# Attention and a feed-forward layer on one core: the second stage by 1024 tokens, with seven block products in place of eight and weights read from DRAM

## The chip, the cores and the metric

The kernel runs on one core of a Trainium2 chip. The metric is the device time of one execution in microseconds; three runs of the kernel before stand here, and their median is the time before. Engines are named as in the profile: PE (TensorE, matmuls), PEld (its weight loads), DVE (VectorE), ACT (ScalarE), POOL (GpSimd), SP (SyncE, which here only issues DMAs). ACT and POOL can issue DMAs too; those instructions stand in the engine's own queue, behind and ahead of its other work.

## What is computed

```python
# attention: batch 8, heads 8, 576 positions, head size 64, band of 64
scores = scale * q @ k.T                       # scale = 1/8
scores = where(0 <= pos_i - pos_j < 64, scores, -1e9)
attn = exp(scores - max(scores)); attn = attn / (sum(attn) + 1e-9)
x = (attn @ v) as (8 * 576 tokens, 512)
# feed-forward
h = x @ w_in                                   # 512 -> 2048
out = maximum(0.01 * h, h) @ w_out             # 2048 -> 512
```

All in fp32; w_in and w_out come as 64-bit floats, handed over as integers. There are 4608 tokens.

## The kernel before

**Feed-forward.** The tokens are nine chunks of 512 (`CH`), and d_ff is 16 blocks of 128 (`FT`, index f). Every fp32 operand of these two products is split in a high and a low part of the type f32r, and one product is three matmuls: high by high, high by low, low by high. A step (c, f) is `mm1` (L529: 4 × 3 = 12 matmuls 128x512 at L539 into one PSUM bank h) and `mm2` (L574: 12 matmuls at L586, three for each of the four accumulators, 128 tokens each, that stay in PSUM for all 16 f). Between the two stand `leak` (ACT, L544, the leaky ReLU out of PSUM), `high` (ACT, L550, the cast to f32r) and `low` (DVE, L554, the rest). `mm2` of a step is issued behind `mm1` of the next. `evict` (L597) moves the four sums out; SP writes them.

**Weights.** Each of the 32 blocks comes as 512 KB of 64-bit words (tile `raw`, the issue at L175 on ACT's queue, the first three on SP's) and is turned into singles by DVE and ACT, step by step: `bits`, `sign`, `abs`, `clamp`, `join`, then `split` (L210, high part, ACT) and `rest` (L214, low part, DVE). High and low parts of all 32 stay in SBUF to the end, 4 × 512 singles per partition and f.

**Attention.** A unit m is two blocks of 64 queries with all heads. Scores are computed transposed, keys on partitions, so that the maximum and the sum over the keys go across partitions. In the late loop, for the pair m, m + 1:

- `scores_3` (L467): the scores of a unit on PE, 32 matmuls (L239)
- `shield_3` (L472): scale and mask, DVE, L477, two per unit, out of PSUM
- `most_3` (L481): the maximum by `partition_all_reduce` on POOL, L486, two per unit
- `exps_3` (L489): minus the maximum (DVE, L492), exponential (ACT, L493), two each
- `sums_3` (L495): the sum by the same instruction on POOL, L497, two per unit
- `fold_3` (L499): 1e-9 added and the reciprocal of 128x512 (DVE, L501 to L503)
- `values_3` (L505): attn @ v on PE, 16 matmuls (L512)
- `product_3` (L518), `low_3` (L523): the product with the reciprocals (DVE, L520), cast (ACT, L521) and low part (DVE, L526), straight into x of the chunk in SBUF

**Order.** The opening is a list of names written out by hand (`ORDER`): weight conversion, the first attention units and 19 first steps. Then come 16 jobs, chunks 0 and 1 with f from 8 to 15, with the rest of the conversion woven in. Then the late loop over `steps`, chunks 2 to 8 by 16 f: every eight steps one pair of units is computed, 24 units (12 to 35) in the first 96 steps; the scores of both units stand behind the second of the eight steps, the values of both behind the sixth. Every engine issues in the order of this code.

Chunks 0 and 1, and the attention before unit 12, are the same before and after.

Of the kernel before, what the change touches and what calls it, by code (L numbers as in the profile page):

```python
# [13 lines left out]
F32 = mybir.dt.float32  # L14
# [17 lines left out]
UPC = CH // QB  # L32
UNITS = 2
TURNED = 2 * UPC
PAIRED = 12
PACE = 5
ROOMS = 3
# [35 lines left out]
"""  # L73
KT = DM // P
# [14 lines left out]
def band_attention_ffn(ctx: ExitStack, tc: tile.TileContext, qT, kB, vW, vL, w_in, w_out, eye_mask, out):  # L89
# [3 lines left out]
    xp = ctx.enter_context(tc.tile_pool(name="xp", bufs=2))  # L93
# [7 lines left out]


# [12 lines left out]
    room = [wk.tile([P, 4 * 512], F32, tag=f"late{FT - 1 - i}", bufs=1, name=f"room{i}") for i in range(ROOMS)]  # L115
# [24 lines left out]
    def load_q(m):  # L140
        if m < NU // 2:
            nc.sync.dma_start(q_of(m), qT[m])

    def load_k(m):
        if m < NU // 2:
            nc.sync.dma_start(k_of(m), kB[m])

    def load_v(m):
        if m < NU // 2:
            nc.sync.dma_start(v_of(m), vL[m - PAIRED] if m >= PAIRED else vW[m])  # L150
# [8 lines left out]

    wi = [[const.tile([P, KT, P], F32R, name=f"wi{f}_{i}") for i in range(2)] for f in range(FT - ROOMS)]  # L160
    wo = [[const.tile([P, DM], F32R, name=f"wo{f}_{i}") for i in range(2)] for f in range(FT - ROOMS)]

    def late_weights(f):
        t = wk.tile([P, 4, 512], F32R, tag=f"late{f}", bufs=1, name=f"w{f}")
        wi.append([t[:, i].rearrange("p (a b) -> p a b", a=KT) for i in range(2)])
        wo.append([t[:, 2 + i] for i in range(2)])

# [41 lines left out]
    def split(n):  # L209
        nc.scalar.copy(flat(parts(n)[0]), singles[n])  # L210

# [7 lines left out]
    def x_of(u):  # L219
        c, w = divmod(u, UPC)  # L220
        if c not in xs:
            xs[c] = [xp.tile([P, KT, CH], F32R, tag=f"x{i}", name=f"x{i}_{c}") for i in range(2)]
        return [x[:, :, w * QB : (w + UNITS) * QB] for x in xs[c]]

# [63 lines left out]
    def top(b):  # L288
        if 0 < b < OWN:
            mx = more_mx[b - 1]  # L290
        else:
            mx = wk.tile([P, 512], F32, tag="pT", bufs=1, name=f"mx{b}")
# [98 lines left out]
    def most(u, j):  # L391
        mx = wk.tile([P, 512], F32, tag="pT", bufs=1, name=f"mx{u}_{j}")
# [62 lines left out]
    def open_room():  # L455
# [3 lines left out]
        k = flat(wk.tile([P, NP, 2, D], F32, tag="y", bufs=1, name="late_k").rearrange("p a b c -> p a (b c)"))  # L459
        later.update(e=e, n=n, v=v, k=k.rearrange("p (a b c) -> p a b c", a=UNITS, b=NP))  # L460

# [3 lines left out]
    def scores_3(m):  # L465
        ps = [bank(t, f"s{m}_{j}") for j, t in enumerate((next(of_h), next(of_h)) if m % 2 else "st")]
        quarter_scores(m, ps, False)  # L467
        probs[m] = ps

    def shield_3(m):  # L470
        ps = probs.pop(m)
        a = mask_of(UNITS * m).bitcast(F32)  # L472
        n = a.shape[1]
        a = flat(a)[:, None, :].broadcast_to([P, H // n, n * QB])
        for j in range(2):
            e, s = (x.rearrange("a (b c) -> a b c", c=n * QB) for x in (e_of(m)[:, j], ps[j]))
            nc.vector.scalar_tensor_tensor(e, s, SCALE, a, ALU.mult, ALU.add)  # L477

    def spare(name):
        return wk.tile([P, 512], F32, tag="pT", bufs=1, name=name)  # L480

    def most_3(m):
        for j in range(2):
            b = 2 * (m % 2) + j
            mx = later["n"][:, b - 1] if b in (1, 2) else spare(f"mx{m}_{j}")
            nc.gpsimd.partition_all_reduce(mx, e_of(m)[:, j], P, ReduceOp.max)  # L486
            probs[m, j] = mx

    def exps_3(m):  # L489
        for j in range(2):  # L490
            e = e_of(m)[:, j]
            nc.vector.tensor_tensor(e, e, probs.pop((m, j)), ALU.subtract)  # L492
            nc.scalar.activation(e, e, AF.Exp)  # L493

    def sums_3(m, j):  # L495
        t = probs[m, "sum"] = spare(f"n{m}") if j else later["n"][:, m % 2]
        nc.gpsimd.partition_all_reduce(t, e_of(m)[:, j], P, ReduceOp.add)  # L497

    def fold_3(m):  # L499
        r, t = later["n"][:, m % 2], probs.pop((m, "sum"))  # L500
        nc.vector.tensor_scalar_add(r[64:], t[64:], 1e-9)  # L501
        nc.vector.tensor_scalar_add(r[:64], r[:64], 1e-9)
        nc.vector.reciprocal(r, r)  # L503

    def values_3(m):  # L505
        ps = bank("st"[m % 2], f"o{m}")
        for w in range(UNITS):
            v = v_heads(m, w)
            for p in range(NP):
                for j in range(2):  # L510
                    c = (2 * p + w) * QB
                    nc.tensor.matmul(  # L512
                        ps[64 * j : 64 * j + 64, c : c + QB], v[:, 2 * p + j], e_of(m)[:, j, c : c + QB],
                        start=True, stop=True,
                    )
        probs[m] = ps

    def product_3(m):  # L518
        r = later["n"][:, m % 2]
        nc.vector.tensor_tensor(r, probs.pop(m), r, ALU.mult)  # L520
        nc.scalar.copy(x_of(UNITS * m)[0], r.rearrange("a (b c) -> a b c", b=NP))  # L521

# [4 lines left out]

    g = {}  # L530

    def mm1(c, f, part):

# [270 lines left out]
```

## Time and profile before

| | |
|---|---|
| runs | 897.09, 896.88, 896.97 us (median 896.97) |
| profiled execution, first to last instruction (span) | 895.8 us |
| busy: PE, PEld | 887.6, 730.1 us |
| busy: DVE, ACT, POOL | 498.1, 304.8, 315.0 us |
| granted PE clock | full in all slices |
| moved by DMA | 68.48 MB, 56.43 read from and 11.01 written to DRAM |
| chain that ended last: PE | 98% |

The time of a run is measured around the whole program; the span of the profiled execution is the time from its first to its last instruction, which is 1.2 us less than the median of the runs. Rows that group instructions read: line, engine, operation, output<-inputs, count | busy us, mean ns of one | idle time of that engine just before, and what ended most of it. The chain of waits is followed back from the last instruction; a row there is start, length, engine, tile, line and count. A row of the DMA view reads: issue line and queue, tile, count and nanoseconds of one issue.

### The profile page before, as it was taken

The page shows a single profiled execution, that of the slowest core. Times are in us where ns is not written, and L with a number is a line of the kernel's source. Part 1 is how long each engine was busy: PE and PEld are TensorE (multiplying, and loading weights), DVE is VectorE, ACT ScalarE, POOL GpSimd, SP SyncE. Part 2 cuts the span into 40 slices and gives each one's busy share as a digit, 9 for nine tenths or more (in the row PEclk, how much of TensorE's full clock was granted, in tenths as well). Part 3 has the DMA queues.
Part 4 walks back from the last instruction along what each step waited for, and adds up shares of the span by engine and source line. Part 5 has one row for each costly group of instructions (what it writes and reads, how often), then busy time and mean ns, then how long its engine had stood idle before and what let it go on. Part 6 is the DMA issues. An engine that isn't in the chain of part 4 may idle for free.

```text
span 895.8 us, 16193 instructions
## 1 busy us (share of the span) xinstructions
PE 887.6 (99%) x7018; PEld 730.1 (82%) x7018; DVE 498.1 (56%) x650; ACT 304.8 (34%) x517; POOL 315.0 (35%) x132
## 2 busy tenths in 40 slices
PE   8999999999999999999999999999999999999998
PEld 5887888888888888888888888888888888888886
DVE  7999774597473636465464737373636455461111
ACT  4666554232222333233322242223323322323222
POOL 5332000674351708080625335351708071620000
PEclk9999999999999999999999999999999999999999
DMA  8663623233311111011211121112101211001001
GB/s 326 207 212 121 221 93 120 72 109 129 106 48 45 50 56 62 26 48 71 72 48 48 48 95 48 48 49 87 55 5 64 75 48 48 2 1 48 0 1 48
DMA packets 30359, 68.48 MB, mean 76 GB/s; under 512 B 3024, under 2 KB 3152, under 8 KB 30288
## 3 DMA queue, kind: packets, MB, share of 16 engines
q1 hardware_dynamic: 25824, 51.75, 16.5%
q10 hardware_dynamic: 4464, 15.70, 5.3%
q8 instruction: 55, 0.90, 0.4%
q14 instruction: 16, 0.13, 0.0%
HBM read 56.43 MB, written 11.01 MB: 75 GB/s over the span
## 4 chain that ended last, share of the span: by engine, by line
PE 98%; POOL 0%; DMA 0%; ACT 0%; issue 0%; DVE 0%; ACTq 0%
PE acc L586 45%; PE h L539 44%; PE s L239 4%; PE o L512 3%; PE o L328 1%; PE o L424 0%; DMA k<-kB 0%; PE s L273 0%; PE t L354 0%; PE s L307 0%; POOL mx L293 0%; POOL room L293 0%; DVE e L283 0%; ACT e L314 0%; ACT e L312 0%
## 5 line engine op out<-in xcount | busy, mean ns | idle before, releaser
L539 PE MATMUL h<-x,wi 128*128 128x512 f32 (+1 forms) x1440 | 337.1, 384 | 0.5 <-ACT g L544 0.5
L539 PEld LDWEIGHTS h<-x,wi 128*128 128x128 f32 x1440 | 265.6, 188 | 54.4 <-ACT g L544 0.7
L586 PE MATMUL acc<-wo,gh 128*128 128x512 f32 x936 | 292.6, 394 | 0.0
L554 DVE TENSOR_TENSOR gl<-g,gh 128x512 fp32r<-128x512 f32 (+1 forms) x147 | 107.5, 732 | 332.7 <-ACT gh L550 332.3
L586 PEld LDWEIGHTS acc<-wo,gh 128*128 128x128 f32 x936 | 172.8, 188 | 36.4
L544 ACT ACTIVATE g<-h 128x512 f32<-128x512 f32 (+1 forms) x147 | 86.4, 588 | 330.8 <-PE h L539 324.1
L586 PE MATMUL acc<-wo,gl 128*128 128x512 f32 x468 | 182.4, 390 | 0.0
L486 POOL PARTITION_ALL_REDUCE mx<-e x12 | 21.4, 1782 | 307.6 <-DVE e L477 307.6
L586 PEld LDWEIGHTS acc<-wo,gl 128*128 128x128 f32 x468 | 87.9, 188 | 18.6
L550 ACT CAST gh<-g 128x512 fp32r<-128x512 f32 (+1 forms) x147 | 90.0, 612 | 10.6 <-PE acc L586 6.3
L503 DVE RECIPROCAL late_n<-late_n 128x512 f32<-128x512 f32 x24 | 80.5, 3353 | 0.8
L539 PE MATMUL h<-x,w 128*128 128x512 f32 x324 | 77.8, 389 | 0.0
L539 PEld LDWEIGHTS h<-x,w 128*128 128x128 f32 x324 | 60.8, 188 | 12.6
L586 PE MATMUL acc<-w,gh 128*128 128x512 f32 x216 | 66.7, 390 | 0.0
L497 POOL PARTITION_ALL_REDUCE late_n<-e x12 | 38.8, 3233 | 25.7 <-ACT late_e L493 25.7
L493 ACT ACTIVATE e<-e 128x512 f32<-128x512 f32 x24 | 15.2, 632 | 95.4 <-DVE e L492 95.4
L586 PEld LDWEIGHTS acc<-w,gh 128*128 128x128 f32 x216 | 40.5, 188 | 8.4
L393 POOL PARTITION_ALL_REDUCE mx<-e x8 | 15.2, 1898 | 90.3 <-DVE e L385 87.0
L586 PE MATMUL acc<-w,gl 128*128 128x512 f32 x108 | 42.0, 389 | 0.0
L293 POOL PARTITION_ALL_REDUCE mx<-e x13 | 25.7, 1977 | 45.1 <-ACT e L285 28.3
L497 POOL PARTITION_ALL_REDUCE n<-late_e x12 | 41.5, 3460 | 0.0
L497 POOL PARTITION_ALL_REDUCE late_n<-late_e x12 | 40.9, 3405 | 0.0
(99 smaller groups left out, 825.7 us busy)
## 6 DMA issues: line engine op xcount, KB each, us to landing
q<-qT SPq DMA_DIRECT2D x34, 256.0 KB, 3.4
raw<-w_out ACTq DMA_DIRECT2D x15, 512.0 KB, 3.3
out<-o SPq DMA_DIRECT2D x30, 256.0 KB, 2.1
raw<-w_in ACTq DMA_DIRECT2D x14, 512.0 KB, 3.3
k<-kB SPq DMA_DIRECT2D x25, 256.0 KB, 3.6
v<-vL SPq DMA_DIRECT2D x12, 512.0 KB, 3.8
late_v<-vL SPq DMA_DIRECT2D x12, 512.0 KB, 4.2
v<-vW SPq DMA_DIRECT2D x8, 520.0 KB, 5.6
```

The costliest lines, as they stand in the source:

```text
L239: nc.tensor.matmul(ps[j][t, c : c + QB], k[i][s, p], q[s, w, p], start=not begun and (not more or (w, p) == (0, 0)), stop=not begun and no ...
L293: nc.gpsimd.partition_all_reduce(mx, probs[b], P, ReduceOp.max)
L393: nc.gpsimd.partition_all_reduce(mx, probs_of[:, j], P, ReduceOp.max)
L486: nc.gpsimd.partition_all_reduce(mx, e_of(m)[:, j], P, ReduceOp.max)
L497: nc.gpsimd.partition_all_reduce(t, e_of(m)[:, j], P, ReduceOp.add)
L503: nc.vector.reciprocal(r, r)
L512: nc.tensor.matmul(ps[64 * j : 64 * j + 64, c : c + QB], v[:, 2 * p + j], e_of(m)[:, j, c : c + QB], start=True, stop=True,)
L539: nc.tensor.matmul(ps, a[:, k, :], b[:, k, part], start=n == 0, stop=n == len(terms) - 1)
L544: nc.scalar.activation(t[0], ps, AF.Prelu, alpha=0.01)
L550: nc.scalar.copy(g[c, f, part.start][0][:, part], t[0])
L554: nc.vector.tensor_tensor(lo, t[0], hi.bitcast(F32), ALU.subtract)
L586: nc.tensor.matmul(acc[c, i], a[:, ts], b, start=begin and n == 0, stop=end and n == 2)
```

## The change

Chunks 0, 1 and 2 (`LEAD = 3`) are computed as before, chunk 2 under new lines (`early_first`, `early_second`) and with the order of f turned so that 15, 14, 13 and 12 come first. The other 3072 tokens go in three turns (`NS`) of 1024.

**Seven products.** x of a turn is cut in 2 × 2 blocks (512 tokens by 256 of d_model), w_in for a pair f, f + 8 in 2 × 2 (256 of d_model by 128). The four blocks of h are put together from seven products (Winograd's form of Strassen's scheme), each of 6 matmuls: `product`, L1103. The combinations of x (`x_build`, L936, DVE) and of w_in (`prep`, L1045) are made ahead; those of the products are made by `put` (ACT, L1109) and five additions per f on DVE (`add`, L1112: one operand from PSUM, one from SBUF); then four leaky ReLUs per f on ACT (L1115, `leaky`). An accumulator bank is used again two or three products later, and waits until the addition from it is done. After the eight f come the casts (`high`, L1118), low parts (`low`, L1121, 32 per turn, DVE) and `second`: 2 halves × 16 f × 12 matmuls, as many as before, whose output is transposed (`outT`, put right on the host by a transposition).

**Weights from DRAM.** `split` also stores the single-precision w_in (16 stores of 256 KB, ACT's queue). During the jobs n = 7 to 15, SP stores the parts of the weights that the turns use unchanged (24 × 256 KB and 16 × 512 KB). In chunk 2 and turn 0, ACT's queue reads singles back, DVE and ACT make the combined blocks, and ACT's queue stores them (eight times, L1042 to L1055). The slots in SBUF that had held weights then serve for other things; a ring of four slots of 1 MB is filled by DMAs that POOL issues (`fill`, L1090: 30 per turn, each read by 24 matmuls). Each fill waits until PE is done with the slot.

**Attention through DRAM.** Scores (L268) and values (L849) of units 12 to 35 go one unit at a time. Of the sums over the keys only one row is kept, as 128x8; DVE takes the reciprocals of that (L826, L827), and SP's DMAs write them to DRAM and spread them over the partitions. The products (L860) are stored to DRAM by unit, and x of a turn is read from there. For units 12 to 19 the sum is not on POOL but on PE: four matmuls with ones (`add_of`, L808), copied out by ACT. The loads of q, k and v move from SP's to ACT's queue. All attention ends within turn 0.

**Order.** From chunk 2 on, the order on each engine is set by a planner (`arrange`) that gets each operation with an engine, a cost, what it waits for and a rank, and always issues what is ready first, by rank.

POOL, in the late loop before; L486 is the maximum, L497 the sum of a pair of units:

```order
L497 ISA late_n<-e 128x512 [waits DVE_49,Activation_49,Pool_49]
L497 ISA n_5544<-e 128x512 [waits Activation_49,Pool_49]
L497 ISA late_n<-late_e 128x512 [waits Activation_49]
L497 ISA n_5600<-late_e 128x512 [waits DVE_49,Activation_49]
L486 ISA mx_0_5906<-e 128x512 [waits DVE_49,Pool_49]
```

POOL, in the change, around the end of chunk 2 and the start of turn 0; L787 is a maximum or a sum, L1090 a fill of the ring:

```order
L1090 DMA p_27_3509<-w_first 128x2048 [waits DMAHW0_49,DMAHW1_49,DMASW1_49,PE_49]
L787 ISA g<-late_e 128x512 [waits Activation_49]
L787 ISA late_o_2495<-e 128x512 [waits DMAHW3_49]
L1090 DMA p_28_3600<-w_first 128x2048 [waits DMAHW2_49,DMAHW7_49,DMASW2_49,PE_49]
L787 ISA late_o_2496<-e 128x512 [waits DMAHW7_49]
L787 ISA late_o_2495<-e 128x512 [waits Activation_49]
L1090 DMA p_29_3724<-w_first 128x2048 [waits DMAHW0_49,DMAHW2_49,DMASW3_49,PE_49]
```

Fills now stand between the reduces, about two reduces to a fill, and each waits for PE and for DMAs; a reduce behind it in the queue waits with it.

DVE, in the late loop before: low parts of steps (L554), the reciprocals of a unit (L501 to L503) and its product (L520):

```order
L554 TENSOR_TENSOR gl_12_0_6398<-g_12_0_6395,gh_12_0_6397 128x512
L501 TENSOR_SCALAR late_n<-n_6348 64x512
L502 TENSOR_SCALAR late_n<-late_n 64x512
L503 RECIPROCAL late_n<-late_n 128x512
L554 TENSOR_TENSOR gl_13_0_6434<-g_13_0_6431,gh_13_0_6433 128x512
L520 TENSOR_TENSOR late_n<-o_6437,late_n 128x512
```

DVE, in the change, from the end of chunk 2 into turn 0: the last low parts of x (L955), then additions of the first seven products (L1112) among the steps of attention units (L781 mask, L791 minus the maximum, L860 product, L826 and L827 reciprocals):

```order
L955 TENSOR_TENSOR pfew_3354<-p_23_2886,pfew_3354 128x4x2x128
L791 TENSOR_TENSOR e<-e,late_o_2496 128x512
L1112 TENSOR_TENSOR pxa_30_3976<-m_0_1_3969,pxa_30_3976 128x512
L781 SCALAR_TENSOR_TENSOR e<-s_0_3912,away 128x512
L860 TENSOR_TENSOR late_n<-o_3829,late_n 128x512
L1112 TENSOR_TENSOR pxa_30_3976<-m_0_2_3998,pxa_30_3976 128x512
L781 SCALAR_TENSOR_TENSOR e<-s_1_3913,away 128x512
L1112 TENSOR_TENSOR p_31_4027<-m_0_3_4007,pxa_30_3976 128x512
L791 TENSOR_TENSOR late_e<-late_e,g 128x512
L826 TENSOR_SCALAR c_2423<-c_2423 128x8
L827 RECIPROCAL c_2423<-c_2423 128x8
```

The additions from PSUM stand behind a mask, a subtraction or a product of attention, and x's last low parts directly ahead of the first of them; a reciprocal is one of 128x8 in place of 128x512.

The core of the diff, cut:

```python
+LEAD = 3
+NS = (NCHUNK - LEAD) // 2
+KEPT = 7
...
     def split(n):
         nc.scalar.copy(flat(parts(n)[0]), singles[n])
+        if n % 2 == 0:
+            nc.scalar.dma_start(w_single[n // 2], singles[n])
...
+        if n >= KEPT:
+            for f in kept[(n - KEPT) * len(kept) // (len(jobs) - KEPT) : (n - KEPT + 1) * len(kept) // (len(jobs) - KEPT)]:
+                f()
...
-    steps = [(c, f) for c in range(2, NCHUNK) for f in range(FT)]
-    for n, (c, f) in enumerate(steps):
...
+    def add_of(m):
+        ps = bank("s", f"sum{m}")
+        for c in range(2):
+            for j in range(2):
+                q = 32 * (2 * j + c)
+                nc.tensor.matmul(
+                    ps[q : q + 32, :256], ones(), e_of(m)[:, j, 256 * c : 256 * c + 256], start=True, stop=True,
+                    tile_position=(0, q),
+                )
...
+    def fill(n, of):
+        ring[n] = hold(RING_AT[n % RING], F32R)
+        nc.gpsimd.dma_start(ring[n], of.rearrange("p a b -> p (a b)"))
...
+    def product(n, part, k, name):
+        b, begin = BANK[k], k < 4
+        if begin:
+            tiles[b] = ps_o.tile([P, 512], F32, tag=f"o{b}", name=name)
+        w, x = ring[n][:, 512 * part : 512 * (part + 1)], [x_part(OF_X[k], j) for j in range(2)]
+        terms = [(kt, i, j) for kt in range(2) for i, j in ((0, 0), (0, 1), (1, 0))]
+        for c, (kt, i, j) in enumerate(terms):
+            nc.tensor.matmul(
+                tiles[b], w[:, 256 * i + 128 * kt : 256 * i + 128 * kt + 128], x[j][:, 512 * kt : 512 * kt + 512],
+                start=begin and c == 0, stop=c == len(terms) - 1, skip_group_check=not begin,
+            )
+
+    def add(to, b, x):
+        nc.vector.tensor_tensor(to(), tiles[b], x(), ALU.add)
...
+                M.append(next_main(6 * MM, partial(product, n, p % 4, k, f"m{s}_{f}_{k}"), got, *after, *(x_done if f == 0 else ())))
```

More of the change, by code (lines that the diff above doesn't have):

```diff
@@ L470, in shield_3 @@
[L470 to L503, printed above, removed]
```

559 lines of the change are left out of this document (466 added, 93 removed).

## The prediction

> **What bounds the kernel now.** I read the page first: its totals, its slices and the chain that ended last.
>
> ```profile
> span 895.8 us, 16193 instructions
> PE 887.6 (99%) x7018; PEld 730.1 (82%) x7018; DVE 498.1 (56%) x650; ACT 304.8 (34%) x517; POOL 315.0 (35%) x132
> PE   8999999999999999999999999999999999999998
> PEclk9999999999999999999999999999999999999999
> q1 hardware_dynamic: 25824, 51.75, 16.5%
> q10 hardware_dynamic: 4464, 15.70, 5.3%
> PE 98%; POOL 0%; DMA 0%; ACT 0%; issue 0%; DVE 0%; ACTq 0%
> ```
>
> TensorE (PE) is busy for 887.6 of 895.8 us at the full granted clock, and 98% of the chain is PE itself, so a matmul taken away is time taken away, as long as nothing else becomes late. The two queues moved 67.45 MB in 21.8% of the span, 195 us: about 345 GB/s while they move.
>
> Second, the chain of waits over one pair of attention units in the middle of the late loop (start, length, piece).
>
> ```profile
> 717.12 2.02 PE s L239 x128
> 719.14 2.95 PE acc L586 x12
> 722.09 5.44 PE h L539 x24
> ...
> 735.69 2.72 PE h L539 x12
> 738.41 2.02 PE o L512 x64
> 740.42 2.94 PE acc L586 x12
> ```
>
> Twelve 128x512 matmuls take 2.72 us, 0.2267 us each, back to back. Scores of two units lie alone on PE, 2.02 us, and so do the values of two; the piece behind each takes 2.95 or 2.94 in place of 2.72, so an insertion costs some 0.23 us more than its length.
>
> Third, the groups by line and shape from 300 to 760 us (busy, mean ns | idle before, releaser), which price the other engines' work.
>
> ```profile
> L497 POOL PARTITION_ALL_REDUCE n<-late_e x10 | 34.6, 3460 | 0.0
> L497 POOL PARTITION_ALL_REDUCE late_n<-e x9 | 29.1, 3233 | 19.3 <-ACT late_e L493 19.3
> L486 POOL PARTITION_ALL_REDUCE mx<-e x9 | 16.0, 1782 | 231.0 <-DVE e L477 231.0
> L492 DVE TENSOR_TENSOR e<-e,mx 128x512 f32<-128x512 f32 x9 | 13.8, 1533 | 1.7 <-POOL mx L486 1.7
> L492 DVE TENSOR_TENSOR late_e<-late_e,late_n 128x512 f32<-128x512 f32 x9 | 6.2, 686 | 0.0
> L477 DVE SCALAR_TENSOR_TENSOR e<-s,away 128x512 f32<-128x512 f32 x18 | 11.6, 686 | 16.6 <-PE s L239 16.6
> L520 DVE TENSOR_TENSOR late_n<-o,late_n 128x512 f32<-128x512 f32 x20 | 13.6, 681 | 0.0
> L544 ACT ACTIVATE g<-h 128x512 f32<-128x512 f32 x77 | 45.9, 596 | 179.0 <-PE h L539 178.9
> L554 DVE TENSOR_TENSOR gl<-g,gh 128x512 fp32r<-128x512 f32 x77 | 57.2, 742 | 181.5 <-ACT gh L550 181.4
> ```
>
> **The change, part by part.** *Matmuls.* A turn of 1024 tokens takes 8 f × 7 products × 6 = 336 matmuls for x@w_in, where two chunks took 2 × 16 × 12 = 384; x@w_out keeps its 384. Three turns save 144 × 0.2267 = **−32.6 us**, all of it on the path.
>
> *Attention on PE.* Before, 12 pairs cost 2 × (2.02 + 0.23) = 4.5 us each, 54 us. Now units come one at a time: 48 insertions of half the length with the same joint, 1.01 + 0.23 = 1.24 us, 59.5 us: **+5.6 us**. The sums of eight units move from POOL to PE, 1024 columns each in four matmuls. The trace has no such matmul. By the values' row (32 matmuls of 64 columns, each recorded twice: 2048 columns in 2.02 us) one sum takes 1.01 us; by the scores' row (64 of 64 on quarters of the array: 4096 columns in 2.02) it takes 0.5. The sums lie on four column groups at a time, so they stand nearer to the scores: I take 0.6, eight times, **+4.8 us** (4.0 to 8.1).
>
> So PE's own work falls by 22.2 us. The rest is what PE may now wait for.
>
> *Opening.* Sixteen 256 KB stores of single weights are added to ACT's queue.
>
> ```profile
> 0.00:50.00 50.00, 45.63 (x699) 34.59 (x700) 41.29 (x93) 29.39 (x57) 21.31 (x16) 1.00 0.75 259
> 167.00:226.00 59.00, 59.00 (x544) 48.53 (x543) 45.80 (x45) 18.79 (x32) 37.30 (x14) 1.00 0.33 113
> L175 ACTq DMA_DIRECT2D raw<-w_out x15: 334/334/363, 14.6 to 148.8; - x15
> q<-qT SPq DMA_DIRECT2D x34, 256.0 KB, 3.4
> raw<-w_out ACTq DMA_DIRECT2D x15, 512.0 KB, 3.3
> ```
>
> The first two are windows (PE, weight load, DVE, ACT and POOL busy, clock, DMA share, GB/s). An issue occupies ACT's queue for 0.334 us (third row), so sixteen are 5.3 us at most; ACT is busy for 29 of the first 50 us and hides most, though DVE, at 41, is what feeds PE there, and ACT feeds DVE. I take **+1.5 us** (0 to 5.3).
>
> *Weights to DRAM.* SP stores 14.7 MB beside the last nine of the first sixteen jobs.
>
> ```profile
> 168.51 2.72 PE h L539 x12
> ...
> 226.10 2.72 PE h L539 x12
> ```
>
> From the first of these jobs to the end of the last are 57.6 us. With the 6.5 MB that the window's 113 GB/s already moved, 21.2 MB at 345 GB/s need 61 us: SP's queue runs 3 us late or more, and the loads of late_k and late_v and the attention's small DMAs stand behind it. A late unit moves; PE has other rows to run. **+1 us** (0 to 6).
>
> *End of chunk 2.* Turn 0's first product waits for all of its x: per unit a store, a fetch (nearest row 3.4 us to land), four 256-wide differences, casts and low parts. DVE has in chunk 2 some 92 us of work if each subtraction takes 0.686 (20 low parts at 0.742, 24 + 22 + 9 of a unit at 0.68, 32 + 16 differences at half of that, an estimate, 8 low parts of weights at 1.3, also twice a row, 12 of x at 0.75), and 110 if the 22 subtractions of the maximum take 1.533, in 123 us of PE (396 matmuls, 23 insertions, eight sums). ACT now also issues the loads of q, k and v and the weights' reads and stores, so its casts queue behind those waits, and DVE's low parts behind the casts. With 13 to 31 us to spare over the chunk, but the chain ending last in it, I take one chain link of 3.4 us and a subtraction: **+4 us** (0 to 12, which is three links).
>
> *Turn 0.* It holds 720 matmuls and 25 insertions, 194 us of PE. POOL has 54 reduces at a mean of (1.78 + 3.35)/2 = 2.57, 139 us, and 30 fills of 1 MB, so a fill may hold POOL for (194 − 139)/30 = 1.8 us before POOL is the bound. Each fill waits for PE to let a slot go, and the reduces queued behind it wait too; the subtraction and exponential behind those can be late without harm, since no turn but the next needs their x. DVE has 112 us (40 additions at 0.686, 24 + 26 + 15 of the units, 32 low parts, x of the next turn), or 185 if all of its 86 subtractions from SBUF to SBUF take 0.85 more. How these meet, rows of the timeline show:
>
> ```profile
> 248.18 3.23 POOL L497 PARTITION_ALL_REDUCE late_n<-e  x1 [2.11 <-ACT late_e L493]
> ...
> 249.80 1.17 DVE L554 TENSOR_TENSOR gl<-g,gh 128x512 fp32r<-128x512 f32 x1 [1.84 <-ACT gh L550]
> ...
> 251.31 3.31 POOL L497 PARTITION_ALL_REDUCE n<-e  x1
> ...
> 254.16 0.69 DVE L554 TENSOR_TENSOR gl<-g,gh 128x512 fp32r<-128x512 f32 x1 [3.19 <-ACT gh L550]
> ```
>
> A low part that starts during a reduce can be held (1.17, and 1.533 in the groups), one 2.85 us into a 3.31 us reduce was not (0.69). An addition of a product reads one operand from PSUM, as L477 does, and that ran at 0.686 beside the reduces; but it stands in DVE's queue behind subtractions that are held. PE can go on for two products, 2.72 us, before it needs the bank that an addition empties. A hold of 0.85 with a subtraction of 0.69 is within that; two in a row are not. I take **+3 us** (0 to 20). The Trainium skill, "SBUF — State Buffer", section "Who interferes with whom", has it that a VectorE instruction with two SBUF inputs and a GpSimd one that reads SBUF exclude each other by a lock, and its summary says that one fully blocks. The trace agrees with the exclusion (1.533 against 0.686) but not for a whole reduce (0.69 at 254.16); by the page a subtraction caught at random would lose half a reduce, 1.3 us in place of 0.85, the term would be 4.6, and the time 886.4 us.
>
> *Turns 1 and 2.* No attention is left, 163 us of PE each; DVE has some 100 instructions. **+0.5 us** for joints (0 to 3). A fill serves 24 matmuls, 5.44 us. At 345 GB/s its 1.05 MB take 3.0 us, so it is hidden with 2.4 us to spare in each.
>
> **The sum.** −32.6 + 5.6 + 4.8 + 1.5 + 1 + 4 + 3 + 0.5 = −12.2 us against the profiled 895.8: a span of 883.6. The median of the runs, 896.97 (897.09, 896.88, 896.97), is 1.2 us above the span, so the time is **884.8 us**.
>
> **The rivals.**
>
> *Fills set the pace (slower).* No row shows a DMA issued by POOL, nor one that writes f32r from f32. If a 1 MB fill keeps the queue for more than 5.44 us, PE waits at every slot of all three turns, and this decides the sign from 5.44 + 12.2/90 = 5.6 us on. At twice the 345 GB/s price, 6.1 us, it costs 90 × (6.1 − 5.44) = 59 us, of which the sum's turn terms are part: about 940 us. For it: the 512 KB rows need 3.3 us to land, little faster than 256 KB, so a part is fixed; POOL is also occupied by reduces, so issues come late. Against: that fixed part overlaps, as the 345 GB/s show, and the ring of four holds three fills ahead. The Trainium skill, "DMA: Bandwidth & Descriptors", section "Measured (HBM→SBUF, 128 partitions, SWDGE, issued from GpSimd)", gives for 1 MB both 6.15 us and 341 GB/s; by the first an estimate is 90 × 0.71 = 64 us and this rival holds, by the second, 3.1 us, it does not. No run here shows which.
>
> *DVE is held in turn 0.* If the 26 subtractions of the maximum are each held by 0.85 us with an addition behind them on which PE waits, the term is 22 in place of 3: 903.8 us, and half of it, 892.8. For it: in the order, additions of the products stand between subtractions and low parts, and POOL reduces in 139 of 194 us. Against: the 2.72 us of slack, and that the rows of late_e show half of these subtractions not held at all.
>
> *Everything hides.* All waits at nothing and the sums at 0.5 give −32.6 + 5.6 + 4.0 = −23 us, 874.0. For it: PE waits for nothing now with the same engines 35 to 56% busy. Against: the join at the end of chunk 2 and the crowded turn 0 have no like in this trace.
>
> That the change does not do its seven products is excluded: 3312 wide matmuls stand in its program where 3456 stood.
>
> **How the numbers follow.** Forecast 0.55, hidden 0.17, DVE held 0.15, fills 0.13. 0.2% is 1.8 us, about what a measurement of this kernel can tell: 895.2 to 898.8 is no change. Forecast and hidden are faster, of the third 0.05 is faster, 0.06 the same, 0.04 slower, and the fills are slower: 0.77, 0.06, 0.17. The range starts at 873.5, half a microsecond under the hidden case, since PE has little idle time now that could vanish, and ends at 899.0, inside the held case; what is beyond is the fills and the upper part of that case, 0.17.
>
> **What would show it.** Right: PE's busy time near 865 us, waits of PE gathered at the end of chunk 2 and in turn 0, few in turns 1 and 2, and fills landing several microseconds ahead of their matmuls. Fills wrong: turns 1 and 2 longer than 163 us each, with PE's idle time ended by POOL's queue, a gap at each fourth product. DVE wrong: in turn 0 idle time of PE ended by additions, with subtractions over 1.5 us in front of them. Stores or x wrong: a PE gap over 12 us before the first product, or late_k, late_v landing after the time of use. The prediction as a whole falls if PE's matmuls themselves no longer take 0.2267 us, or if the time is above 899.

## The result, and the profile after

The changed kernel takes 969.95 us (median of 4 runs, 965.0 to 973.42) against 897.03 us (median of 4, 896.88 to 897.14): 1.081 times as long, interval 1.078 to 1.084. The forecast was 884.8 us. The profiled execution has a span of 971.7 us; 75.9 us more than before.

The page of the changed kernel, the lines that answer to those of before:

```profile
span 971.7 us, 17011 instructions
PE 904.4 (93%) x6938; PEld 724.8 (75%) x6938; DVE 537.9 (55%) x847; ACT 332.7 (34%) x565; POOL 312.5 (32%) x206
PE   9999999999978876699888988989999999999998
PEclk9999999999999888799899989999999999999999
q0 software_dynamic: 12960, 94.38, 29.1%
q1 hardware_dynamic: 84960, 62.44, 21.3%
q10 hardware_dynamic: 28688, 55.55, 18.0%
...
p<-w_second POOLq DMA_DIRECT2D x48, 1024.0 KB, 5.3
p<-w_first POOLq DMA_DIRECT2D x42, 1024.0 KB, 5.1
```

PE is no longer busy throughout: in twelve of the slices 12 to 27 it falls to six to eight tenths, and in six of those its granted clock falls to seven or eight tenths. No other engine has become the bound. The queues now move 212 MB in place of 67, 94 of them by a third queue, POOL's fills, which land in 5.1 and 5.3 us (the last two rows).

The slices lie in two stages. The windows of the changed kernel for chunk 2, for turn 0, for turn 1 and for turn 2 (length, then busy PE, PEld, DVE, ACT, POOL; clock, DMA share, GB/s):

```profile
225.52:399.27 173.75, 137.45 (x1614) 105.26 (x1612) 101.28 (x164) 52.87 (x91) 56.40 (x30) 0.90 0.80 247
399.27:636.62 237.35, 213.33 (x1875) 169.74 (x1873) 143.48 (x200) 68.82 (x116) 153.73 (x84) 0.95 0.75 225
...
636.62:802.94 166.32, 166.32 (x720) 136.35 (x721) 66.33 (x105) 53.45 (x87) 15.30 (x29) 0.99 0.66 216
802.94:967.74 164.80, 164.80 (x721) 134.93 (x719) 52.38 (x77) 46.56 (x76) 14.25 (x27) 1.00 0.55 186
```

Turns 1 and 2 do what the seven products promise: no idle time, 166 and 165 us, where two chunks of before take 64 pieces of 2.72 us, 174 us. Chunk 2 begins at 225.5, where before it began at 226.1, so the opening and the stores of weights cost nothing. All that is lost lies in chunk 2, 173.8 us where the forecast had 127, and in turn 0, 237.4 where it had 197. PE stands idle for 36.3 and 24.0 us there, and part of the rest is matmuls at half the clock.

The waits of PE in the changed kernel, over the whole span (us in total, times, longest):

```profile
PE s L268 <- DVE late_e L781: 13.9, 6, 7.6
PE s L268 <- DVE e L781: 9.2, 6, 2.9
PE acc L984 <- ACT gs L1008: 7.2, 2, 6.6
PE s L268 <- ACT late_n L856: 7.1, 4, 6.5
PE s L268 <- ACT g L815: 5.3, 1, 5.3
PE o L849 <- ACT e L795: 4.6, 3, 2.2
PE sum L808 <- ACT late_e L795: 3.6, 1, 3.6
```

Of these, the seven largest, all but the third row stand at attention's insertions: the scores of a unit (L268) wait for the banks that DVE or ACT has yet to empty, the values (L849) and sums (L808) for an exponential. Rows of the timeline at one such gap in turn 0, DVE first, then PE:

```profile
505.20 0.69 DVE L860 TENSOR_TENSOR late_n<-o,late_n 128x512 f32<-128x512 f32 x1 [5.91 <-DMA late_n<-rows]
505.81 0.68 DVE L1112 TENSOR_TENSOR pxa<-m,pxa 128x512 f32<-128x512 f32 x1
506.41 0.68 DVE L781 SCALAR_TENSOR_TENSOR e<-s,away 128x512 f32<-128x512 f32 x1
507.24 0.33 PE L268 MATMUL s<-q,k 64*64 64x64 f32 x1 [2.81 <-DVE e L781]
```

DVE stands 5.91 us before a product L860 whose reciprocals have not come back from DRAM. Behind it in DVE's queue are an addition of the seven products and the mask of the next unit, both ready; PE's scores wait for the bank that the mask empties. Over turn 0 this wait is the largest that DVE has (first row; the second is the landing of the DMA that it waits for, in the DMA view of the same stretch):

```profile
DVE late_n L860 <- DMA late_n<-rows: 33.5, 8, 8.8
...
late_n<-rows SPq DMA_DIRECT2D x30, 128.0 KB, 5.1
```

In chunk 2 the same happens on ACT. Its rows ahead of PE's gap of 5.30 us at 290.64, and that of PE:

```profile
279.19 0.68 ACTq L164 DMA_DIRECT2D v<-vL  x1
282.66 0.35 ACTq L156 DMA_DIRECT2D q<-qT  x1
286.77 0.35 ACTq L160 DMA_DIRECT2D k<-kB  x1
287.24 0.89 ACTq L1042 DMA_DIRECT2D p<-w_single  x2
288.17 1.04 ACT L1048 CAST p<-p 128x1024 fp32r<-128x1024 f32 x1 [8.89 <-DMA q<-qT]
...
290.21 0.38 ACT L815 COPY g<-sum 128x256 f32<-128x256 f32 x1
290.64 0.85 PE L268 MATMUL s<-q,late_k 64*64 64x64 f32 x3 [5.30 <-ACT g L815]
```

From 279.9 to 287.2 ACT does little but wait to issue DMAs. The copy L815 that would free PE's bank stands behind them.

### The profile page after: what moved, and what is told of

Same layout as the page of the kernel before. It is cut to its first block, busy times and chain, and to the rows that moved or that the text cites. A ratio compares the mean times of both kernels' runs of the same rounds, so it can differ in the third digit from the quotient of the medians.

```text
span 971.7 us, 17011 instructions
## 1 busy us (share of the span) xinstructions
PE 904.4 (93%) x6938; PEld 724.8 (75%) x6938; DVE 537.9 (55%) x847; ACT 332.7 (34%) x565; POOL 312.5 (32%) x206
## 5 line engine op out<-in xcount | busy, mean ns | idle before, releaser
L1103 PE MATMUL m<-pfew,p 128*128 128x512 f32 x720 | 173.2, 396 | 1.8 <-DVE pxa L1112 1.8
L1103 PEld LDWEIGHTS m<-pfew,p 128*128 128x128 f32 x720 | 136.4, 191 | 31.3 <-DVE pxa L1112 2.2
L1128 PE MATMUL y<-gs,p 128*128 128x512 f32 x576 | 140.1, 396 | 0.4 <-ACT p L1131 0.4
L1128 PE MATMUL y<-pxa,p 128*128 128x512 f32 x576 | 140.5, 400 | 0.0
L1128 PEld LDWEIGHTS y<-pxa,p 128*128 128x128 f32 x576 | 110.8, 193 | 24.4
L1128 PEld LDWEIGHTS y<-gs,p 128*128 128x128 f32 x576 | 107.4, 187 | 26.6 <-ACT p L1131 0.8
L787 POOL PARTITION_ALL_REDUCE late_o<-e x40 | 96.0, 2415 | 90.7 <-DVE e L781 36.8
L787 POOL PARTITION_ALL_REDUCE g<-late_e x40 | 97.5, 2454 | 41.0 <-DVE late_e L781 15.6
L1090 POOL DMA_DIRECT2D p<-w_second x48 | 25.6, 534 | 181.2 <-PE y L1128 136.7
L1115 ACT ACTIVATE p<-p 128x512 f32<-128x512 f32 x63 | 39.7, 631 | 127.8 <-DVE p L1112 127.8
L1090 POOL DMA_DIRECT2D p<-w_first x42 | 22.5, 537 | 180.5 <-PE m L1103 115.0
L1103 PE MATMUL m<-pxb,p 128*128 128x512 f32 x288 | 74.2, 406 | 2.5 <-DVE p L1131 2.5
L1112 DVE TENSOR_TENSOR p<-m,pxa 128x512 f32<-128x512 f32 x63 | 43.4, 690 | 54.5 <-PE m L1103 53.6
L1112 DVE TENSOR_TENSOR pxa<-m,pxa 128x512 f32<-128x512 f32 x57 | 39.3, 689 | 60.0 <-PE m L1103 54.7
L1103 PEld LDWEIGHTS m<-pxb,p 128*128 128x128 f32 x288 | 56.2, 197 | 15.1 <-DVE p L1131 2.9
L1121 DVE TENSOR_TENSOR gs<-p,gs 128x512 fp32r<-128x512 f32 x48 | 38.2, 796 | 50.3 <-ACT gs L1118 50.2
L554 PE MATMUL acc<-p,gs 128*128 128x512 f32 x264 | 64.8, 395 | 0.0
L268 PE MATMUL s<-q,k 64*64 64x64 f32 x1648 | 43.6, 239 | 18.7 <-DVE late_e L781 10.7
L268 PEld LDWEIGHTS s<-q,k 64*64 64x64 f32 x1648 | 37.4, 151 | 28.5 <-issue 11.9
L554 PEld LDWEIGHTS acc<-p,gs 128*128 128x128 f32 x264 | 49.0, 188 | 10.7
L1121 DVE TENSOR_TENSOR pxa<-p,pxa 128x512 fp32r<-128x512 f32 x36 | 29.5, 818 | 43.4 <-ACT pxa L1118 43.4
L1118 ACT CAST gs<-p 128x512 fp32r<-128x512 f32 x48 | 29.6, 619 | 68.5 <-PE y L1128 68.4
```

Of the source, the lines that this page charges most:

```text
L268: nc.tensor.matmul(ps[j][t, c : c + QB], k[i][s, p], q[s, w, p], start=not begun and (not more or (w, p) == (0, 0)), stop=not begun and no ...
L554: nc.tensor.matmul(acc[c, i], a[:, ts], b, start=begin and n == 0, stop=end and n == 2)
L787: nc.gpsimd.partition_all_reduce(sum_of(m, j), e_of(m)[:, j], P, what)
L1090: nc.gpsimd.dma_start(ring[n], of.rearrange("p a b -> p (a b)"))
L1103: nc.tensor.matmul(tiles[b], w[:, 256 * i + 128 * kt : 256 * i + 128 * kt + 128], x[j][:, 512 * kt : 512 * kt + 512], start=begin and c == ...
L1112: nc.vector.tensor_tensor(to(), tiles[b], x(), ALU.add)
```

## The experiments

The theories are those of the first expectation. Q: ready work stands in in-order queues behind instructions that wait for a DMA. D: chunk 2 and turn 0 hold too much work for DVE and POOL. F: the fills in POOL's queue hold up the reduces. T is the form that Q took later: the fills' traffic makes the attention's own DMAs land late. The table gives the time, and for chunk 2 and turn 0 the length with PE's idle time in brackets (length less PE's busy time, from the windows of each). In the expectations idle time was summed from the gaps of the timeline, 36 and 21 us.

| kernel | time | chunk 2 | turn 0 |
|---|---|---|---|
| the change | 969.95 | 173.8 (36.3) | 237.4 (24.0) |
| x_norm | 927.29 | 154.4 (20.1) | 208.2 (6.7) |
| x_issue | 962.33 | 158.3 (23.6) | 238.2 (25.2) |
| x_spread | 975.97 | 152.0 (22.3) | 223.7 (26.6) |
| x_land | 937.04 | 158.8 (26.5) | 216.4 (13.8) |
| x_lag | 953.62 | 163.0 (30.9) | 229.5 (20.5) |
| x_local | 984.40 | 222.5 (72.2) | 200.0 (6.9) |
| x_nofill | 934.66 | 171.3 (34.5) | 202.0 (1.8) |
| x_noprep | 959.85 | 148.6 (17.0) | 242.1 (26.1) |
| x_smallfill | 934.94 | 170.3 (33.6) | 204.4 (3.1) |
| x_spfill | 946.25 | 173.5 (33.7) | 210.8 (8.9) |
| y_order | 931.60 | 165.1 (28.1) | 206.1 (6.1) |
| x_normprep | 901.64 | 134.5 (7.0) | 204.8 (3.5) |

Single times of the change differ by up to 8 us, and each other kernel ran once, so differences under about 10 us between these times are not read. In all but x_nofill and x_smallfill the planner also lays the work out anew, so a unit or more may move from one stage to the other: x_issue, x_lag, x_noprep and x_normprep have the scores of one unit less in chunk 2 and of one more in turn 0. x_issue, x_local and x_spfill compute some wrong values, and the cause is open; the number and size of their instructions and transfers are as described, but a missing wait cannot be excluded, so they bear less weight.

**x_norm: no way through DRAM for the reciprocals.**

```python
-        nc.vector.tensor_tensor(n_of(m), x, r_of(m), ALU.mult)
+        nc.vector.tensor_scalar(n_of(m), x, 0.02, None, ALU.mult)
# and without the steps c, c0, c1, I, rows and spread
```

> Left out: the normalisation of units 12 to 35. Their products L860 multiply by a constant, and the sums' way through DRAM (compact, reciprocal, rows, spread) is gone; the sums themselves stay. The changed kernel loses 58 us of PE idle time (36 in chunk 2, 21 in turn 0) and some 36 us more at half the granted clock behind the idle spells. Theory Q (work stands in in-order queues behind instructions that wait for a DMA: DVE's L860 for the spread rows, ACT's casts for its own DMA issues): turn 0's idle time falls from 21 to under 6 us and with it the half-clock time, chunk 2 keeps 25 us or more of idle time since its ACT queue is unchanged; time 925 to 940. Theory D (attention is packed too densely into chunk 2 and turn 0: POOL's and DVE's own work decides): under 10 us fall, 960 or more. Theory F (fills in POOL's queue hold up the reduces): the same, 960 or more.

Turn 0's idle time fell from 24.0 to 6.7 us, just above Q's 6, and its length by 29; so the way of the reciprocals, on which L860 waits, decides there, as Q has it, against D and F. Chunk 2 fell by 19 us too, to 20.1 us of idle time where Q had 25 or more: there also DVE had stood before L860, for 16.5 us in all, which Q had left out.

**x_issue: ACT issues no bulk DMA.**

```python
-        return op("ACT", 0.1, fn, *after, rank=rank, lag=1.5, land=2.2 + kb / 200.0)
+        return op("SP", 0.08, fn, *after, rank=rank, us_more=kb)
# and nc.sync in place of nc.scalar for q, k, v, L1042 and L1055
```

> All bulk DMAs of chunk 2 and turn 0 that ACT issues (q, k, v, the weights' reads and stores) go on SP's queue. Theory Q: ACT no longer stands behind waiting issues, chunk 2's 36 us of idle time falls to under 20, time 930 to 950, unless SP's small DMAs now stand behind the bulk ones, which would show as longer waits of L860 for its rows and give 960 to 990. Theories D and F: no fall in chunk 2's idle time, 960 to 975.

Chunk 2 lost 15 us and its idle time fell to 23.6, not under 20; the time, at 962, misses Q's band and lies in those of the rivals. D and F, which had no fall in chunk 2, do not fit either, and the sign of SP's bulk DMAs in the way, longer waits of L860 for its rows, is not there: in turn 0 DVE stood 33.9 us before it, 48.9 in the change. What ACT's issues cost is not shown by this run, because the edit also tells the planner that these transfers occupy SP's wire, and the order of all engines changes. In x_land, below, ACT issues them all as before, and another order alone brings chunk 2 to 158.8 us, the same.

**x_spread: the later units wait for points spread over turns 0 and 1.**

```python
+    def gate_at(s, k):
+        if s < NS - 1:
+            at[PAIRED + UPC * (s + 1) + k]["S"]["after"].append(main)
# called at f = 0, 2, 4, 6 of the products and at four steps of the second product
```

> Same work, but the scores of units 20 to 27 wait for eight points spread over turn 0, those of units 28 to 35 for eight points of turn 1; chunk 2 keeps units 12 to 19 alone. Theory D: idle time near nothing in turns 0 and 1 (under 5 us), in chunk 2 under 12; time 890 to 905. Theory Q: turn 0 and 1 lose their idle time too, since a unit's waiting instructions are far from the next unit's, but chunk 2 keeps 20 us or more, as ACT's issues of weights and loads still wait there; 905 to 930. Theory F: turns 0 and 1 keep half of it, 935 or more.

D falls; F's marks, half of the idle time kept and 935 or more, are met, and x_smallfill below decides on F. Turn 0 holds the scores and values of eight units, where it held eleven scores and fourteen values, and its idle time is still 26.6 us; turn 1, idle-free before, now has 12.9 (204.5 us long, PE busy 191.6). Each unit brings its stall along, wherever it is put. Q's band was missed as well: it had supposed that distance between units would help. It does not: the planner still counts on early rows, and DVE waited for them before L860 nearly as long as before, in half as many units (from 377 to 601 us):

```profile
DVE late_n L860 <- DMA late_n<-rows: 35.8, 8, 8.0
```

**x_land: the planner is told later landings.**

```python
-        return op("SP", 0.08, ...)                          # and ACT: 0.1, land=2.2 + kb / 200.0
+        return op("SP", 0.55, ...)                          # and ACT: 0.45, land=5.0 + kb / 200.0
-                x["end"] = max(wire, t) + 2.2
+                x["end"] = max(wire, t) + 5.0
```

> Same work, same queues; only three numbers of the planner change: a DMA of SP lands after 5.0 us in place of 2.2 and costs its queue 0.55 in place of 0.08, a bulk DMA of ACT lands 2.8 us later and costs 0.45 in place of 0.1. So the order puts waiting instructions later. Theory Q: idle time of 58 us falls by half or more, time 915 to 940. Theory D: the work is as dense as before, 955 to 975. Theory F: fills and reduces keep their order, 955 or more.

The span fell by 36.5 us with nothing but another order (the time by 33 against the median of the change), 21 in turn 0 and 15 in chunk 2. So the loss is one of order against landing time, and not of work. Idle time fell by a third, from 60 to 40 us, not by half. The rows of L840 landed in the same 5.1 us as in the change, so the landings did not get better; the order got them into account.

**x_lag: only L860 and the reciprocals are put later.**

```python
+ lag=4.0 on inverse_of, lag=8.0 on product_of
```

> Same work and queues; the planner adds 8 us before it puts a unit's product L860, and 4 us before its reciprocal, so that on DVE they stand behind work of later units that is ready. Nothing else is told to it. Theory Q (an instruction in DVE's queue that waits for a DMA holds up the next unit's mask and subtraction): turn 0's idle time falls from 21 to under 8 us, chunk 2 keeps 20 to 30 through ACT's queue; time 930 to 945. Theory F (fills and reduces share POOL's queue, and reduces come late): turn 0 keeps 15 us or more, 955 to 975.

This misses Q's band, and turn 0 keeps 20.5 us of idle time, which is F's mark there (15 or more). L860 no longer appears among DVE's waits in turn 0. PE's values wait instead (from 389 to 618 us; first the waits, then DVE's L860 and PE's values at two of the four gaps):

```profile
PE o L849 <- issue: 4.9, 2, 2.5
...
PE o L849 <- ACT gs L1118: 4.0, 1, 4.0
PE o L849 <- ACT p L1115: 3.9, 1, 3.9
...
460.60 0.68 DVE L860 TENSOR_TENSOR late_n<-o,late_n 128x512 f32<-128x512 f32 x1
461.38 1.83 PE L849 MATMUL o<-e,v 128*64 128x64 f32 x32 [3.88 <-ACT p L1115]
...
557.46 0.68 DVE L860 TENSOR_TENSOR late_n<-o,late_n 128x512 f32<-128x512 f32 x1
558.24 1.15 PE L849 MATMUL o<-e,v 128*64 128x64 f32 x32 [2.37 <-issue]
```

The releasers that the profile names are not the holders. Each of the four gaps, 12.8 us in all, ends 0.10 us behind an L860. That product also empties the bank into which the values of the unit after the next go: in the planner's list, values wait for the product of two units before. Put 8 us later, it no longer holds up DVE, but PE. So this run does not speak against Q or for F: the one instruction that waits for the rows is itself waited for, and cannot be moved freely.

**x_local: the reciprocals on DVE again, 128x512, no DRAM.**

```python
-        c = compact[m % 2]
-        nc.vector.tensor_scalar_add(c, c, 1e-9)
-        nc.vector.reciprocal(c, c)
+        r = r_of(m)
+        for j in range(2):
+            h = slice(64 * j, 64 * j + 64)
+            nc.vector.tensor_scalar_add(r[h], sum_of(m, j)[h], 1e-9)
+        nc.vector.reciprocal(r, r)
```

> One part undone: the normalisation of units 12 to 35 is again reciprocals of 128x512 on DVE with sums from POOL alone (none on PE); products still go to DRAM for x. DVE has 24 x 3.35 = 80 us more to do, POOL 16 reduces more in chunk 2. Theory Q: with no DRAM round trip ahead of L860 turn 0's idle time is under 10 us although DVE has more work, chunk 2's under 25; time 920 to 940. Theory D (too dense): more work on DVE and POOL makes it worse, 970 or more. Theory F: 955 or more.

Chunk 2 went as D has it: 222.5 us, in which DVE is busy for 197.7 us, 89%, 43.6 of them the thirteen reciprocals, and POOL for 155.3. There is no room on DVE for reciprocals in chunk 2, so the way through DRAM had a use there. Turn 0 has Q's 6.9 us of idle time in 200.0, but it holds the scores of 8 units and the values of 9, where the change has 11 and 14, so this does not decide between Q and D.

**x_nofill and x_smallfill: no fills, and fills of a sixteenth of the bytes.**

```python
+        if n < RING:
             nc.gpsimd.dma_start(ring[n], of.rearrange("p a b -> p (a b)"))
```

```python
+        k = 2048 if n < RING else 128
+        nc.gpsimd.dma_start(ring[n][:, :k], of.rearrange("p a b -> p (a b)")[:, :k])
```

> Left out: all fills of the ring but the first four, so the turns multiply by wrong weights; POOL has 86 instructions less and 90 MB less are moved. Theory F: reduces no longer wait behind fills, turn 0's idle time falls from 21 to under 8, 935 to 945. Theory Q: DVE still waits for the rows, only their DMAs land faster without the fills' traffic (the landings of 5 us go to about 3.5): turn 0 keeps 10 us or more, chunk 2 changes by less than 5; 945 to 965.

> Left out: of each fill behind the first four only a sixteenth of the bytes is moved, so the turns multiply by wrong weights; the fills stand in POOL's queue as before, wait for PE as before and hold back the reduces behind them as before. Without any fills turn 0's idle time fell from 21 to 2 us and the spread rows landed in 2.9 us in place of 5.1. Theory T (the fills' traffic makes the attention's own DMAs land late, and those are what the order has no room for): idle time of turn 0 under 6 us, rows land in about 3 us, time 935 to 942. Theory F (the fills' place in POOL's queue): 15 us or more are left, 955 or more.

Without fills turn 0 lost nearly all of its idle time, which F had forecast and Q had not. The second kernel tells why: every fill stays at its place in POOL's queue, PE, DVE and SP go through the same instructions in the same order as in the change, only the bytes are fewer, and turn 0 has 3.1 us idle. So with this order the traffic makes the loss, as T has it, and the place in POOL's queue alone does not. The rows for L860 in that kernel, from 395 to 600 us, to be held against 5.1 us in the change:

```profile
late_n<-rows SPq DMA_DIRECT2D x30, 128.0 KB, 3.0
```

With 123 GB/s moved in turn 0 in place of 225 the three DMAs in a row ahead of every L860 land sooner: the sums in 3.0 and 3.2 us in place of 4.5 and 4.8, the reciprocals in 2.0 in place of 3.2, the rows in 3.0 in place of 5.1, some 5 us a unit. The Trainium skill, "DMA: Bandwidth & Descriptors", section "Issuing engines are not separate DMA queues", says that DMAs issued from different engines run on the same 16 DMA engines and interleave; the trace agrees, with 5.1 against 3.0 us for SP's DMAs by what POOL issues beside them.

**x_spfill: SP issues the fills.**

```python
-        nc.gpsimd.dma_start(ring[n], of.rearrange("p a b -> p (a b)"))
+        nc.sync.dma_start(ring[n].bitcast(F32), of.rearrange("p a b -> p (a b)"))
```

> The fills are issued by SP in place of POOL, as many bytes. Theory F: POOL's reduces stand behind nothing that waits for PE, turn 0's idle time under 8 us, 940 to 955. Theory T: the traffic is the same and turn 0 keeps 12 us or more; SP's own small DMAs now stand behind fills that wait for PE, which can only add to it; 960 to 985.

8.9 us of idle time were left in turn 0: just above F's bound and below T's 12, and the time is in F's band. The traffic is no less, 251 GB/s, and the rows land no sooner, 5.2 us. But this run does not show that freeing POOL's queue helps. The edit also books each fill with 1024 KB on SP's wire, so the planner counts on later landings of SP's DMAs, as in x_land, and sets another order: DVE stood only 6.4 us before L860 in turn 0, 48.9 in the change. That F is not needed is seen in y_order, below: there the fills stand in POOL's queue as in the change, at 257 GB/s, and another order leaves 6.1 us.

**x_noprep: no combined blocks of w_in.**

```python
-                    n, got = filled(w_first[p // 4], *made_before)
+                    n, got = filled(w_second[p // 4 % 8], *made_before)
# and no reads, differences, casts and stores of the blocks
```

> Left out: the combined blocks of w_in (their reads, differences, casts and stores in chunk 2), and the fills of w_in read other weights in their place, as many bytes. Theory Q, its ACT part: ACT's queue loses 48 DMA issues and 8 casts, and what stood behind their waits is on time: chunk 2's idle time falls from 36 to 10 to 20 us, turn 0's stays about 20; time 935 to 950. If the q, k and v issues are what holds ACT, chunk 2 keeps 28 us or more and the time is 960 or more.

Chunk 2 fell to 148.6 us with 17.0 idle, in the band; the time, 959.85, did not reach its own, since turn 0 and turn 1 took 5 and 7 us longer. Which part of the combined blocks holds up chunk 2 is not shown: with ACT's issues and casts the edit takes 24 us of DVE's work out of it, and the traffic falls from 247 to 192 GB/s.

**x_normprep: both left out.**

> Left out: the normalisation's way through DRAM and the combined blocks of w_in, both together (each alone brought chunk 2 from 174 to 154 and 149 us). If each holds up chunk 2 by a wait of its own, the two add: 125 to 137 us with under 10 us of idle time, and 900 to 915 in all. If another wait, such as the loads of q, k and v or the stores and fetches of x, stands behind both, chunk 2 stays at 145 or more, and the time at 920 or more.

The two add, as had been expected. Chunk 2 takes 134.5 us with 7.0 idle:

```profile
227.19:361.71 134.52, 127.52 (x1549) 98.96 (x1547) 77.50 (x104) 45.47 (x83) 54.55 (x30) 0.96 0.62 195
361.71:566.50 204.79, 201.34 (x1943) 161.00 (x1937) 140.22 (x171) 67.90 (x115) 153.00 (x83) 1.00 0.80 250
```

This is close to what the forecast had for the whole change, 127 and 197 us, and it leaves out work. It takes 901.64 us, so even then the change does not gain.

**y_order: a more thorough order.**

```python
+    tuned = {"sub": (0.9, None, 0.7), "spread_of": (0.15, None, None), ...}   # rank, lag, cost
-                x["end"] = max(wire, t) + 2.2
+                x["end"] = max(wire, t) + 5.4
```

> Same work and queues as the changed kernel; the planner is told that SP's DMAs land after 5.4 us in place of 2.2, ACT's 2.5 us later than it had them at 0.8 us of its queue each, and six ranks, three lags and two costs are set anew. Theory T with Q (late DMAs ahead of work in in-order queues): turn 0's idle time under 5 us with a length below 200, chunk 2 at 145 to 160 us since there the chain of DMAs of the last units is itself longer than the matmuls beside it; time 905 to 930. Theory F: turn 0 keeps 10 us, 940 or more.

Turn 0 came down to 206.1 us with 6.1 idle, chunk 2 only to 165.1; the time was 931.6. All marks of T with Q are just missed, and F's, 10 us and 940 or more, by more. In turn 0, 5.3 of the 6.1 us are again values that start 0.10 us behind an L860. Of the kernels that do all the work this has the lowest time, with x_land within the noise, and it is 4% slower than the kernel before. None of these runs beats the kernel before.

## Why the prediction was wrong

**Right.** The count of the products: turns 1 and 2 run at 166 and 165 us with no idle time, and the bare sum of their matmuls was 163. The sums on PE: eight recorded matmuls of a unit take 0.64 us in the timeline, 0.6 was taken. The fills do not set the pace: their median landing is near to the 5.44 us that a fill serves, but they overlap, and PE waits for none of them in turns 1 and 2. The opening and the stores were costed at 2.5 us and took nothing. The rival that DVE is held by POOL is there (L791 took 1.27 and 1.00 us on average in its two groups in turn 0) but does not decide: only 1.8 us of PE's waits in turn 0 end with an addition, and x_smallfill has 1.02 and 1.11 us for L791 and 3.1 us of idle time.

**The step that failed.** "A late unit moves; PE has other rows to run", and for turn 0 "can be late without harm, since no turn but the next needs their x". PE has no other rows: its queue is in order, and the scores, sums and values of the units stand in it at fixed places. A unit that is late by 5 us stops PE there. And what makes it late are DMAs: the change put five in a row on the path of every unit (sums out, reciprocals out, rows back, then store and fetch of x). The sum has one link of 3.4 us for them, of an uncrowded stretch, at the end of chunk 2; for the three that every L860 waits for it has nothing, in either stage. In turn 0 they take 3.2 to 5.1 us each, and instructions that wait for them stand in DVE's queue ahead of other units' work. That the order is at fault is shown by x_land, which changes nothing else and takes 15 and 21 us off the two stages; that in turn 0 the order fails because of late landings, by x_smallfill, which changes nothing but the traffic; that in chunk 2 the way of the reciprocals and the combined blocks make up 39 us of the loss of 51, by x_normprep.

**The terms.** The end of chunk 2 was put at +4 us (0 to 12) and cost 47 more; turn 0 at +3 (0 to 20) and cost 40 more; the rest of the 88 us between the forecast span of 883.6 and 971.7 is turns 1 and 2 with their joints, some 4, less what the opening did not take. Turn 0's bare length was itself some 5 to 7 us short: in x_smallfill and x_normprep, with hardly any idle time, it takes 204 to 205 us less 3, not 194, and at most 3 of these 7 went to the clock. PE's busy time, the first sign named, is 904.4 us in place of 865, for this and for the clock, below. One sum was off as well: the terms listed for DVE in chunk 2 add up to 88 us, not 92; nothing hung on it.

**The idle time is not all of it.** In the two stages PE was idle for 60 us, and the stages are 94 us longer than the bare 123 and 194. Windows of the changed kernel at the gap that ends at 290.64, and at two shorter gaps, 421.6 to 423.4 and 300.3 to 302.5 (the column before the last two is the granted clock):

```profile
284.92:288.34 3.42, 0.42 (x2) 0.00 (x0) 0.00 (x0) 0.17 (x1) 0.00 (x0) 1.00 0.21 40
288.34:295.17 6.83, 4.51 (x69) 3.82 (x70) 4.51 (x9) 3.75 (x7) 0.00 (x0) 0.50 1.01 306
295.17:298.58 3.41, 3.41 (x48) 2.36 (x47) 3.38 (x6) 0.00 (x0) 3.01 (x2) 1.00 0.98 253
...
421.47:424.88 3.41, 1.60 (x7) 1.05 (x6) 3.31 (x6) 0.70 (x2) 2.29 (x2) 1.00 0.58 165
424.88:428.29 3.41, 3.41 (x68) 2.92 (x68) 1.75 (x3) 2.09 (x4) 1.72 (x1) 0.50 0.91 278
428.29:431.70 3.41, 3.41 (x16) 2.81 (x16) 1.58 (x4) 1.70 (x3) 1.51 (x1) 1.00 0.41 154
...
298.58:301.99 3.41, 1.70 (x10) 1.05 (x6) 0.76 (x2) 0.98 (x2) 0.62 (x1) 1.00 0.49 127
301.99:305.40 3.41, 2.73 (x70) 2.31 (x71) 2.65 (x5) 2.95 (x6) 0.00 (x0) 1.00 0.75 239
```

After the gap of 5.3 us the clock is 0.50 for 6.8 us, of which the last 4.5 lie behind the gap, and matmuls there take about twice as long (the scores of a unit 2.5 us in place of 1.2), so the gap cost some 2.3 us more than its length. Over chunk 2 and turn 0, PE worked 19.7 and 25.2 us at half the clock, and lost half of that, 10 and 13 us. The forecast priced a wait by its length alone.

**What stays open.** In x_normprep 11 us over the bare 123 are left in chunk 2: 7.0 are idle time, most of it before the second product's matmuls (L980), which wait 5.0 us for low parts on DVE, and 4 went to the clock; why those low parts are late is open. What of chunk 2's loss in the change is due to ACT's queue, to DVE's work on the combined blocks or to the traffic is not separated. Nor is it shown whether POOL's queue adds to the lateness in turn 0 of the change: no run frees it and keeps both the order and the traffic.

## What to carry to other kernels

An engine that is busy for 98% of the time is not safe from latency: its own queue is in order, so every result that it is to take up at a fixed place has to be early, and an order laid out for one landing time has to be laid out again when the transfers beside it triple. Before moving a step of a chain through DRAM, count the DMAs in a row on one unit's path, price them at the landing time of the crowded stage, and look at who stands behind the instruction that waits for the last of them, and at who waits for what that instruction frees. A wait on PE costs its length and, where it is long enough, a stretch at half the clock behind it.

## What the runs showed of the hardware

The granted clock of PE fell to 0.50 3.0 us into the idle spell from 285.34 to 290.64 us and came back 4.5 us after work was taken up (0.50 from 288.34 to 295.17). Shorter spells are uneven: one of 1.8 us (from 421.6) was followed by a clock of 0.50 from 424.88 to 428.29, one of 2.2 us (from 300.3) by none. Of the eight spells over 1.5 us within turn 0, seven were followed by such a stretch. The Trainium skill, "TensorE: Matmul & The Clock Gate", section "Why this matters for your kernels", asks for no idle gaps of PE over some 3 us; the spell at 421.6 shows that a shorter one can do. The Trainium skill, "TensorE: Matmul & The Clock Gate", section "What's actually happening", has the clock go by a window of some 3.4 us that runs freely. The trace agrees: all thirteen stretches at half the clock between 288 and 640 us last 3.41 us or two or three times that, and their starts lie whole multiples of 3.41 us apart (288.34 and 424.88, forty; 424.88 and 465.84, twelve). The spell at 421.6 lies within one such step, 421.47 to 424.88, of which PE worked 1.60 us; the one at 300.3 lies across two.

A DMA of 128 KB from DRAM to SBUF landed in a median of 5.1 us beside 1 MB fills, and in 3.0 us beside fills of 64 KB, at a mean of 225 and 123 GB/s moved. The mean rate does not fix it: in x_lag, with 1 MB fills and 235 GB/s, the same rows landed in 3.7 us.
